# Full-height kv sums and a newly searched instruction order in a fused linear-attention and FFN kernel

## The chip, the cores and the metric

The kernel runs on one core of a Trainium2 chip. The metric is device time in microseconds (us); a median over several executions is given. Times of one kernel scatter by up to about 2 us either way, and the clock granted to TensorE, which differs from run to run, has a part in it: of eleven runs of the kernel before on one chip, the five with a mean clock of 0.989 or more took 262.73 to 264.61 us, the six with 0.985 or less 264.16 to 266.26. Kernels are compared by ratios: the mean time of one kernel's fast runs over that of the kernel before in the same rounds on the same chip, with a 95% interval. Such a ratio is not quite the ratio of the medians that stand beside it.

## The reference, cut to what matters

```python
def attn(q, k, v):                     # (8 batches, 8 heads, 576 tokens, 64)
    q_p, k_p = phi(q), phi(k)          # phi(x) = max(x + 1, min(exp(x), 1))
    kv  = einsum('bhsd,bhse->bhde', k_p, v)
    z   = k_p.sum(axis=2)
    return einsum('bhsd,bhde->bhse', q_p, kv) / (einsum('bhsd,bhd->bhs', q_p, z)[..., None] + 1e-6)
x = attn(q, k, v), as 4608 tokens x 512
out = (((x @ w1) * (x @ w2)) @ w3) @ w_out
```

All inputs and the output are float32. The 576 tokens of a batch are four tiles of 128 ("J") and a remainder of 64 ("R").

## The kernel before

The program is one list of short tokens, ORDER. Every engine executes its own instructions in the order in which the tokens emit them, so the list fixes what stands in front of what on each engine. Letters that this text uses:

- L, M, N: loads of k, q, v of a batch (`M1.2`: all of batch 1's q except the remainder). A gate such as `M1.2<E3` holds a load back until another has landed. B, C, E: loads of w1/w2, w_out and w3, cast to bf16 on the way, from the POOL (GpSimd) queue. The other loads are issued by SyncE (SP).
- x, y, z (for k) and X, Y, Z (for q): exp on ScalarE (ACT), min and max on VectorE (DVE). v: cast of v.
- K: one kv sum for four heads. A: the attention output of one batch, in parts. a, b: q transposes on TensorE (PE) and their copy.
- w: transposes of a w3 piece on PE and the copy out of PSUM, the memory that PE writes to here; a unit on PE waits until a bank of it is free. U, W: the product w3 @ w_out, halves and whole, with a copy at the end of W.
- F: one 128-column unit of the FFN (8 matmuls of 512 columns, a copy on ACT, a product on DVE). O, S: output matmuls and stores.
- A token that ends in "+" makes its copy on DVE in place of ACT. For K it meant, in this kernel, the half-height version; on the load of a remainder it means the POOL queue.

The two ways to form kv (cut):

```python
    def kv_half(b, g):
        ...
        for i in range(2):                      # two head pairs
            steps = [... four tiles, halves (0, 1) ...]
            steps.append((... remainder ..., (g,)))
            for n, (kk, vv, halves) in enumerate(steps):
                for r in halves:                # rows 0-63 into bank 0, rows 64-127 into bank 1
                    rows = slice(r * R, (r + 1) * R)
                    nc.tensor.matmul(kvp[:, r, i * W:(i + 1) * W], kk[rows], vv[rows], ...)
        nc.scalar.copy(out=kvf, in_=kvp[:, 0, 0:2 * W])
        nc.vector.tensor_tensor(out=kvs[b][...], in0=kvf, in1=kvp[:, 1, 0:2 * W], op=ALU.add)

    def kv_full(b, g):
        ...
        rows = slice(g * R, (g + 1) * R)
        for i in range(2):
            for j in range(NJ):                 # four 128-row tiles
                nc.tensor.matmul(kvp[:, 0, i * W:(i + 1) * W], kj[:, hp, j]..., vt[:, j, ...]...,
                                 start=(j == 0), stop=False)
            nc.tensor.matmul(kvp[:, 0, i * W:(i + 1) * W], kr[rows, i * P:(i + 1) * P],
                             vr[rows, 2 * i:2 * i + 2, :]..., start=False, stop=True)
```

A half-height unit is 18 matmuls of 64 rows, a copy and an add. A full-height one is 8 matmuls of 128 rows and 2 of 64, and one copy. Going from 128-row to 64-row matmuls and back is what the texts below call a change of (tiling) mode.

Of the kernel before, what the change touches and what calls it, by code (L numbers as in the profile page):

```python
# [13 lines left out]
P = 128  # L14
# [4 lines left out]
def kernel(  # L19
# [158 lines left out]

    kvs, qts, xns = {}, {}, {}

    def kv_half(b, g):


        kj, kr = ph["k", b]
        if g == 0:
            kvs[b] = att.tile([P, KC, 2, D + 1], BF16, tag="kv", name="kv")
        kvp = at_ps.tile([P, 2, 512], F32, tag="at", name="kvp")
        W = 2 * (D + 1)
        for i in range(2):
            hp = 2 * g + i  # L190
            steps = [(kj[:, hp, j].rearrange("p u d -> p (u d)"),
                      vt[:, j, 2 * hp:2 * hp + 2, :].rearrange("p h e -> p (h e)"), (0, 1))
                     for j in range(NJ)]
            steps.append((kr[:, i * P:(i + 1) * P],
                          vr[:, 2 * i:2 * i + 2, :].rearrange("p h e -> p (h e)"), (g,)))
            for n, (kk, vv, halves) in enumerate(steps):
                for r in halves:
                    rows = slice(r * R, (r + 1) * R)
                    nc.tensor.matmul(  # L199
                        kvp[:, r, i * W:(i + 1) * W], kk[rows], vv[rows],  # L200
                        start=(n == 0), stop=(n == (NJ if r == g else NJ - 1)))
        kvf = lr.tile([P, 2 * W], F32, tag="kvf", name="kvf")
        nc.scalar.copy(out=kvf, in_=kvp[:, 0, 0:2 * W])
        nc.vector.tensor_tensor(
            out=kvs[b][:, 2 * g:2 * g + 2].rearrange("p a u e -> p (a u e)"), in0=kvf,
            in1=kvp[:, 1, 0:2 * W], op=ALU.add)

    def kv_full(b, g):

        kj, kr = ph["k", b]  # L210
        if g == 0:
            kvs[b] = att.tile([P, KC, 2, D + 1], BF16, tag="kv", name="kv")
        kvp = at_ps.tile([P, 2, 512], F32, tag="at", name="kvp")
        W = 2 * (D + 1)
        rows = slice(g * R, (g + 1) * R)
        for i in range(2):
            hp = 2 * g + i
            for j in range(NJ):
                nc.tensor.matmul(kvp[:, 0, i * W:(i + 1) * W],
                                 kj[:, hp, j].rearrange("p u d -> p (u d)"),  # L220
                                 vt[:, j, 2 * hp:2 * hp + 2, :].rearrange("p h e -> p (h e)"),
                                 start=(j == 0), stop=False)
            nc.tensor.matmul(kvp[:, 0, i * W:(i + 1) * W], kr[rows, i * P:(i + 1) * P],
                             vr[rows, 2 * i:2 * i + 2, :].rearrange("p h e -> p (h e)"),
                             start=False, stop=True)
        return kvp[:, 0, 0:2 * W]
# [289 lines left out]
    def step(s):  # L516
# [20 lines left out]
        elif t == "U":  # L537
            wf_mm(b, 0)
            held["U", b] = True
        elif t == "W":  # L540
            wf_mm(b, 1 if ("U", b) in held else 2, alt)
        elif t in "LMN":
            name = "kqv"["LMN".index(t)]
            ins = load_qkv(name, src[name], b, i, alt)
            loaded(s, ins)
        elif t == "B":
            for ins in load_w12(b):
                loaded(s, ins)
        elif t == "C":
            loaded(s, load_wo(b))  # L550
        elif t == "E":
            loaded(s, load_w3(b))
        elif t in "xX":
            phi_exp("kq"["xX".index(t)], b, i)
        elif t in "yY":
            phi_min("kq"["yY".index(t)], b, i)
        elif t in "zZ":
            phi_max("kq"["zZ".index(t)], b, i)
        elif t == "v":
            v_unit(b, i, alt)  # L560
        elif t == "T":
            qt_load(b, i)
        elif t == "K":
            if alt:
                kv_half(b, i)
            else:
                kv_copy(b, i, kv_full(b, i))
        elif t == "A":
            nat_units(b, ((0, 1), (2, 3), (4,))[i])
        elif t == "D":  # L570
            xt_load(b, i)
        elif t == "P":
            xt_tr(b, i, alt)
        elif t == "a":
            held["a", b, i] = q_tr(b, i)
        elif t == "b":
            held["a", b, i](alt)
        elif t == "c":
            held["c", i] = kv_full(0, i)
        elif t == "d":  # L580
            first_kvz(i, held["c", i])
        elif t == "e":
            held["e", i] = first_nd(i, i < 2)
        elif t == "f":
            held["e", i][0]()
        elif t == "g":
            held["e", i][1]()
        elif t == "h":
            if i == 0:
                held["h"] = [f_open(0, 0), f_open(0, 1)]  # L590
            for f in range(2):
                for ps, w in zip(held["h"][f], (w1_sb, w2_sb)):
                    f_mm(0, f, ps, w, i)
        elif t == "i":
            f_close(0, i, *held["h"][i])
        elif t == "r":
            first_rest()
# [32 lines left out]
```

## Time and profile before

263.69 us (263.31 to 264.38, 3 runs).

| engine | busy us of 263.1 | what matters |
|---|---|---|
| PE | 240.0 | full from 58 us to the end; one wide gap, 47 to 52 us |
| DVE | 171.4 | not waited for after 58 us |
| ACT | 124.9 | executes in order; holds PSUM banks while it waits for a load |
| DMA | full to about 52 us | the casting weight queue and the loads of q, k, v share it |

Busy time alone would say that DVE and ACT have room and that PE has 23 us to spare. The view to trust is the one by stretches: it tells in which part of the time PE is full. Columns: stretch and its length, then busy us and instructions of PE, PE's weight loads, DVE, ACT and POOL, then clock, DMA share, GB/s.

```profile
60.00:258.00 198.00, 198.00 (x1399) 94.13 (x1393) 140.60 (x358) 94.57 (x158) 0.00 (x0) 1.00 0.68 177
```

PE is busy for 198.00 of 198.00 us. Here a microsecond of work taken from DVE or ACT is worth nothing, and one added to PE is paid. The groups that the change takes off DVE and ACT are these (busy us, mean ns, then the idle time before them):

```profile
L204 DVE TENSOR_TENSOR kv<-kvf,kvp 128x260 bf16<-128x260 f32 x13 | 5.5, 419 | 4.2 <-ACT kvf L203 4.2
L203 ACT COPY kvf<-kvp 128x260 f32<-128x260 f32 x13 | 4.9, 375 | 6.2 <-PE kvp L199 6.2
```

### The profile page before, as it was taken

The page shows a single profiled execution, that of the slowest core. Times are in us where ns is not written, and L with a number is a line of the kernel's source. Part 1 is how long each engine was busy: PE and PEld are TensorE (multiplying, and loading weights), DVE is VectorE, ACT ScalarE, POOL GpSimd, SP SyncE. Part 2 cuts the span into 40 slices and gives each one's busy share as a digit, 9 for nine tenths or more (in the row PEclk, how much of TensorE's full clock was granted, in tenths as well). Part 3 has the DMA queues.
Part 4 walks back from the last instruction along what each step waited for, and adds up shares of the span by engine and source line. Part 5 has one row for each costly group of instructions (what it writes and reads, how often), then busy time and mean ns, then how long its engine had stood idle before and what let it go on. Part 6 is the DMA issues. An engine that isn't in the chain of part 4 may idle for free.

```text
span 263.1 us, 4457 instructions
## 1 busy us (share of the span) xinstructions
PE 240.0 (91%) x1652; PEld 115.7 (44%) x1652; DVE 171.4 (65%) x431; ACT 124.9 (47%) x199; POOL 13.5 (5%) x30
## 2 busy tenths in 40 slices
PE   0467999399999999999999999999999999999993
PEld 0133544255544554454444544444444444444442
DVE  0495644465898996988798679669886624433341
ACT  1576521663885986497345743733242222323200
POOL 2075300000000000000000000000000000000000
PEclk9999999869999999999999999999999999999999
DMA  5999999957959989997999897993655411202033
GB/s 174 293 322 195 206 208 256 264 175 225 368 162 283 188 222 229 324 209 185 283 181 229 227 338 231 176 244 78 135 156 171 94 50 34 88 0 80 0 122 121
DMA packets 75045, 49.51 MB, mean 188 GB/s; under 512 B 39568, under 2 KB 69520, under 8 KB 75024
## 3 DMA queue, kind: packets, MB, share of 16 engines
q1 hardware_dynamic: 68448, 43.85, 62.1%
q0 software_dynamic: 6432, 5.24, 12.6%
q8 instruction: 13, 0.21, 0.3%
q10 hardware_dynamic: 144, 0.13, 0.1%
q14 instruction: 8, 0.07, 0.1%
HBM read 38.80 MB, written 9.44 MB: 183 GB/s over the span
## 4 chain that ended last, share of the span: by engine, by line
PE 83%; DMA 11%; SPq 2%; ACT 1%; POOL 1%; issue 1%; ACTq 0%
PE a_ps L371 24%; PE o_ps L390 23%; PE b_ps L371 23%; DMA q<-in_q_dram 5%; PE wf_ps L464 3%; PE kvp L199 3%; DMA w_sb<-in_moe_w_dram 3%; DMA k<-in_k_dram 3%; PE nd L265 3%; SPq L111 1%; PE xtp L285 1%; SPq L120 1%; PE w3p L454 1%; PE o_ps L417 1%; PE tp L309 1%
## 5 line engine op out<-in xcount | busy, mean ns | idle before, releaser
L371 PEld LDWEIGHTS <-w_sb 128*128 128x128 bf16 x576 | 54.3, 98 | 64.1 <-DMA w_sb<-in_moe_w_dram 0.7
L377 DVE TENSOR_TENSOR ab<-a_sb,b_ps 128x512 bf16<-128x512 f32 x72 | 49.0, 684 | 41.0 <-PE b_ps L371 35.5
L371 PE MATMUL a_ps<-xt,w_sb 128*128 128x512 bf16 x288 | 75.1, 380 | 0.0
L371 PE MATMUL b_ps<-xt,w_sb 128*128 128x512 bf16 x288 | 74.9, 379 | 0.2 <-DMA w_sb<-in_moe_w_dram 0.2
L376 ACT COPY a_sb<-a_ps 128x512 f32<-128x512 f32 x72 | 41.9, 585 | 61.8 <-PE a_ps L371 59.8
L390 PE MATMUL o_ps<-wf_sb,ab 128*128 128x512 bf16 x280 | 63.9, 379 | 0.0
L390 PEld LDWEIGHTS <-ab 128*128 128x128 bf16 x280 | 26.5, 98 | 30.5 <-DVE ab L377 0.2
L393 DVE COPY o_sb<-o_ps 128x512 f32<-128x512 f32 x20 | 13.8, 688 | 15.1 <-PE o_ps L390 15.1
L162 DVE SCALAR_TENSOR_TENSOR kj<-k,e 128x256 bf16<-128x256 f32 x64 | 23.5, 416 | 0.0
L162 DVE SCALAR_TENSOR_TENSOR qj<-q,e 128x256 bf16<-128x256 f32 x64 | 23.5, 416 | 0.1
L137 ACT ACTIVATE e<-q 128x1024 bf16<-128x1024 f32 x16 | 16.8, 1059 | 10.8 <-DMA q<-in_q_dram 10.8
L393 ACT COPY o_sb<-o_ps 128x512 f32<-128x512 f32 x15 | 8.8, 585 | 22.8 <-PE o_ps L390 18.5
L275 DVE TENSOR_TENSOR xn<-nd,r 128x512 bf16<-128x512 f32 x28 | 18.0, 685 | 0.0
L141 DVE TENSOR_SCALAR e<-e 128x1024 bf16<-128x1024 bf16 x32 | 13.1, 417 | 7.3 <-ACT e L137 7.3
L464 PE MATMUL wf_ps<-wo_sb,w3t 128*128 128x512 bf16 x64 | 17.1, 411 | 0.1
L137 ACT ACTIVATE e<-k 128x1024 bf16<-128x1024 f32 x16 | 16.9, 1057 | 0.3 <-DMA k<-in_k_dram 0.3
L171 ACT CAST vt<-v 128x1024 bf16<-128x1024 f32 x13 | 13.7, 1050 | 1.3 <-DMA v<-in_v_dram 1.3
L100 PE MATMUL warm<-zero 128*128 128x512 bf16 x12 | 4.2, 523 | 10.2 <-DVE zero L94 10.2
L141 DVE TENSOR_SCALAR er<-er 128x256 bf16<-128x256 bf16 x16 | 3.5, 218 | 9.2 <-ACT er L137 9.2
L464 PEld LDWEIGHTS <-w3t 128*128 128x128 bf16 x64 | 6.2, 104 | 7.1 <-issue 1.5
L199 PEld LDWEIGHTS <-kj 64*128 64x128 bf16 x208 | 6.6, 94 | 4.8 <-issue 4.2
L199 PE MATMUL kvp<-vt,kj 64*128 64x130 bf16 x208 | 8.7, 218 | 0.0
(79 smaller groups left out, 153.3 us busy)
## 6 DMA issues: line engine op xcount, KB each, us to landing
out_dram<-o_sb SPq DMA_DIRECT2D x31, 256.0 KB, 3.0
k<-in_k_dram SPq DMA_DIRECT2D x7, 1024.0 KB, 7.8
q<-in_q_dram SPq DMA_DIRECT2D x7, 1024.0 KB, 8.3
v<-in_v_dram SPq DMA_DIRECT2D x6, 1024.0 KB, 6.9
v<-in_v_dram SPq DMA_DIRECT2D x4, 512.0 KB, 8.1
w3b<-in_moe_w_dram POOLq DMA_DIRECT2D x8, 256.0 KB, 13.1
w_sb<-in_moe_w_dram POOLq DMA_DIRECT2D x8, 256.0 KB, 9.0
out_dram<-o_sb SPq DMA_DIRECT2D x9, 128.0 KB, 2.4
```

The lines of the kernel that those rows point to most:

```text
L137: nc.scalar.activation(out=e, in_=x, func=AF.Exp)
L141: nc.vector.tensor_scalar_min(out=e, in0=e, scalar1=1.0)
L162: nc.vector.scalar_tensor_tensor(out=out, in0=x, scalar=1.0, in1=e, op0=ALU.add, op1=ALU.max)
L171: copy_of(alt)(out=vt[:, :, 4 * i:4 * i + 4, 0:D], in_=raw["v", b].rearrange("p (h j d) -> p j h d", h=H, j=NJ)[:, :, 4 * i:4 * i + 4])
L199: nc.tensor.matmul(kvp[:, r, i * W:(i + 1) * W], kk[rows], vv[rows], start=(n == 0), stop=(n == (NJ if r == g else NJ - 1)))
L275: nc.vector.tensor_tensor(out=dst.rearrange("p (c u) e -> p u c e", u=2), in0=v4[:, :, :, 0:D], in1=r[0:n].unsqueeze(3).to_broadcast([n, 2 ...
L371: nc.tensor.matmul(ps, w[:, kc, f * P:(f + 1) * P], xt[:, 4 * c:4 * c + 4, kc, :], start=(kc == 0), stop=(kc == KC - 1))
L376: nc.scalar.copy(out=a_sb, in_=a_ps)
L377: nc.vector.tensor_mul(out=abs_[c][:, f, :], in0=a_sb, in1=b_ps)
L390: nc.tensor.matmul(o_ps, ab[:, f, m * P:(m + 1) * P], wf_sb[:, f, :], start=(f == 0), stop=(f == FC - 1))
L393: copy_of(alt)(out=o_sb, in_=o_ps)
L464: nc.tensor.matmul(wfs[i], w3ts[i][:, kc, :], wo_sb[:, kc, :], start=(kc == 0), stop=(kc == FC - 1))
```

## The change

Its intent: every kv unit as full-height matmuls with a single copy, which puts one copy in place of a copy and an add, and a new order, found by a search whose transfer rates came from traces in which two DMA queues work at once. The core of the diff (the order itself is 28 lines, cut):

```diff
-    def kv_half(b, g):
-        ...
-            if alt:
-                kv_half(b, i)
-            else:
-                kv_copy(b, i, kv_full(b, i))
+            kv_copy(b, i, kv_full(b, i), alt)
     ORDER (after the first w3 and FFN units)
-    i0.0 i0.1 x1.1 w1+ F0.2 F0.3 N1.3 w2+ y1.0 F0.4 N1.1 y1.1 F0.5 U1 N2.3 U0 W0+ E4 x1.2 W1 w3+
-    W2+ W3 M2.3 z1.0 X1.0 E5 M0.3 y1.2 z1.1 Y1.0 Z1.0 Z1.1 X1.1 Y1.1 M2.2 z1.2 F0.6 E6 w4 Z1.2
-    Z1.3 z1.3 F0.7 E7 w5 Z1.4 a1.0 v1.2+ b1.0 z1.4 U4 w6 W4 ...
+    x1.2 w1 Z1.4 x1.1 F0.2 y1.0 z1.0 M2.3+ F0.3 F0.4 B3 y1.1 w2 U0 F0.5 z1.1 N1.0 E4 U1 N2.3
+    X1.0 z1.2 W0+ N1.3+ w3+ X1.1 E5 W1+ y1.2 W2 Y1.0 Z1.0 Z1.1 v1.2+ W3 N1.1 F0.6 w4+ M2.2 F0.7
+    Y1.1 L2.3 a1.0 M3.3 w5+ b1.0 M0.3 z1.3 E6 U4 z1.4 w6 v1.0 W4+ E7 Z1.2 Z1.3 w7+ U5 W5 K1.0+ ...
-    GATES = "B0<M0.1 C0<L0.1 E0<L0.1 E4<N0.1 M1.2<E3 N1.0<B3"
+    GATES = "B0<L0.0 C0<L0.0 E0<N0.1 M1.2<E3 N1.0<B3"
```

More of the change, by code (lines that the diff above doesn't have):

```diff
@@ L179 @@
     kvs, qts, xns = {}, {}, {}
-    def kv_half(b, g):
-        kj, kr = ph["k", b]
-        if g == 0:
-            kvs[b] = att.tile([P, KC, 2, D + 1], BF16, tag="kv", name="kv")
-        kvp = at_ps.tile([P, 2, 512], F32, tag="at", name="kvp")
-        W = 2 * (D + 1)
-        for i in range(2):
-            hp = 2 * g + i
-            steps = [(kj[:, hp, j].rearrange("p u d -> p (u d)"),
-                      vt[:, j, 2 * hp:2 * hp + 2, :].rearrange("p h e -> p (h e)"), (0, 1))
-                     for j in range(NJ)]
-            steps.append((kr[:, i * P:(i + 1) * P],
-                          vr[:, 2 * i:2 * i + 2, :].rearrange("p h e -> p (h e)"), (g,)))
-            for n, (kk, vv, halves) in enumerate(steps):
-                for r in halves:
-                    rows = slice(r * R, (r + 1) * R)
-                    nc.tensor.matmul(
-                        kvp[:, r, i * W:(i + 1) * W], kk[rows], vv[rows],
-                        start=(n == 0), stop=(n == (NJ if r == g else NJ - 1)))
-        kvf = lr.tile([P, 2 * W], F32, tag="kvf", name="kvf")
-        nc.scalar.copy(out=kvf, in_=kvp[:, 0, 0:2 * W])
-        nc.vector.tensor_tensor(
-            out=kvs[b][:, 2 * g:2 * g + 2].rearrange("p a u e -> p (a u e)"), in0=kvf,
-            in1=kvp[:, 1, 0:2 * W], op=ALU.add)
     def kv_full(b, g):
@@ L470 @@
     ORDER = """
-    I1 L0.0 L0.3 M0.0 I0 M1.3 X0.0 x0.2 N0.0 y0.2 N0.3 z0.4 v0.0 M0.1 I2 L0.1 E0 E1 x0.0 X0.1
-    N0.1 Y0.0 Z0.0 B0 X1.2 Z0.1 y0.0 z0.0 z0.1 Y0.1 v0.2+ x0.1 H12 Y1.2 L1.3 B1 c0.0 B2 L1.2
-    Z0.2 a0.0 E2 b0.0 d0.0 e0.0 y0.1 Z0.3 z0.2 a0.1 b0.1+ z0.3 e0.1 v0.1 C0 E3 f0.1 w0+ f0.0
-    c0.1 C1 g0.1 d0.1 e0.2 f0.2 e0.3 g0.0 f0.3 x1.0 g0.2 g0.3 M1.2 B3 h0.0 h0.1 h0.2 N1.0 h0.3
-    i0.0 i0.1 x1.1 w1+ F0.2 F0.3 N1.3 w2+ y1.0 F0.4 N1.1 y1.1 F0.5 U1 N2.3 U0 W0+ E4 x1.2 W1 w3+
-    W2+ W3 M2.3 z1.0 X1.0 E5 M0.3 y1.2 z1.1 Y1.0 Z1.0 Z1.1 X1.1 Y1.1 M2.2 z1.2 F0.6 E6 w4 Z1.2
@@ L477 @@
-    Z1.3 z1.3 F0.7 E7 w5 Z1.4 a1.0 v1.2+ b1.0 z1.4 U4 w6 W4 v1.0 T1.1 a1.1 v1.1+ U5 L2.3 b1.1
-    N3.3 U6 K1.0+ X2.2 W5+ w7+ K1.1 W6 L2.2 A1.0 U7 x2.2 W7 A1.1 X2.0 O0.3 N2.2 Y2.0 Y2.2 X2.1
-    P1.1+ L3.3 P1.0 Z2.4 Y2.1 X0.2 O0.2+ L3.2 Z2.0 y2.2 M3.3 Z2.1 x2.0 z2.4 P1.3 y2.0 M3.2 P1.2
-    O0.1 x2.1 Z2.2 z2.0 x3.2 v2.0 O0.0+ y2.1 v2.2+ z2.1 Z2.3 T2.0 F1.0 N3.2 Y0.2 z2.2 Z0.4 F1.1
-    v2.1 K2.0+ T0.1 z2.3 x3.0 F1.2 F1.3 y3.0 K2.1+ y3.2 A1.2 F1.4 M4.2 D1.1 z3.0 X3.2 X3.0 Y3.2
-    F1.5 x3.1 A2.0 X3.1 F1.6 P2.0 v3.2 A2.1 v3.0 M4.3 z3.4 S0.3 y3.1 Z3.4 F1.7 Y3.1 T2.1 Y3.0
@@ L483 @@
-    P2.1 r0 z3.1 z3.2 z3.3 Z3.0 O1.1 v3.1 P2.2 L5.3 L4.2 Z3.1 Z3.2 L4.3 O1.3 Z3.3 M5.3 P2.3 X4.0
-    Y4.0 X4.2 K3.0+ F2.0 F2.1 N4.3 A2.2 T3.0 x4.0 S0.2 N4.2 Y4.2 F2.2 X4.1 y4.0 F2.3 S0.1 K3.1+
-    M6.3 F2.4 x4.1 z4.0 x4.2 Z4.0 y4.2 Z4.1 A3.0 y4.1 O1.2 F2.5 Y4.1 O1.0 M5.2 A3.1 S0.0 v4.1
-    P3.1 F2.6 P3.3+ z4.1 v4.0 P3.2 F2.7 z4.4 Z4.4 X5.0 Z4.2 S1.3 T3.1 P3.0 v4.2 Z4.3 z4.2 X5.2
-    O2.3+ Y5.0 D2.1 F3.0 z4.3 L5.2 X5.1 T4.0 A3.2 x5.0 S1.1 S1.2 N5.3 F3.1 N5.2 K4.0+ F3.2 Y5.1
-    x5.1 K4.1+ Z5.0 y5.1 T4.1 L6.2 F3.3 A4.0 O2.0 F3.4 y5.0 x5.2 A4.1 z5.0 L6.3 y5.2 D3.1 O2.1+
@@ L489 @@
-    Y5.2 F3.5 Z5.1 D4.0 S1.0 S2.3 v5.2 A4.2 M6.2 Z5.2 v5.0 F3.6 F3.7 Z5.4 x6.2 O3.3+ Z5.3 v5.1
-    z5.1 T5.1 z5.2 z5.3 O2.2 x6.0 F4.0 z5.4 X6.2 x6.1 T5.0 F4.1 F4.2 K5.0+ y6.0 y6.1 X6.0 Y6.0
-    K5.1+ S2.1 S2.2 z6.0 F4.3 y6.2 S2.0 F4.4 N6.2 F4.5 O3.2 L7.2 Z6.0 X6.1 A5.0 Z6.1 z6.4 z6.1
-    F4.6 Y6.1 v6.1+ F4.7 z6.2 A5.1 S3.2 O3.0+ M7.2 O4.0 v6.0 z6.3 S3.3 Z6.2 O4.1+ L7.3 X7.0 N6.3
-    A5.2 Z6.3 v6.2 x7.0 x7.2 X7.1 O4.3+ O3.1 D5.0 Y6.2 S3.0 O4.2+ T6.0 y7.0 y7.2 x7.1 Y7.0 K6.0+
-    F5.0 F5.1 z7.4 N7.2 F5.2 Z6.4 N7.3 K6.1+ S4.3 z7.0 T6.1 z7.1 F5.3 A6.0 v7.2+ y7.1 F5.4 S4.1
@@ L495 @@
-    D5.1 F5.5 Y7.1 D4.1 A6.1 M7.3 F5.6 F5.7 S4.0 Z7.0 D6.0 z7.2 X7.2 O5.2+ Z7.1 O5.0 v7.0+ Z7.2
-    Y7.2 O5.1+ Z7.3 T7.0 S3.1 A6.2 S5.1 Z7.4 S5.0 T7.1 F6.0 v7.1 K7.0+ D6.1 z7.3 F6.1 F6.2 K7.1+
-    S4.2 O5.3+ S5.3 A7.0 F6.3 S5.2 F6.4 A7.1 F6.5 F6.6 F6.7 A7.2 D7.0 O6.0 O6.3 D7.1 S6.0 O6.1+
-    F7.0 F7.1 O6.2+ S6.2 F7.2 F7.3 F7.4 F7.5 F7.6 F7.7 O7.1+ F8.0 O7.0 S6.1 F8.1 F8.2 S6.3 F8.3
-    F8.4 F8.5 S7.0 F8.6 F8.7 S7.1 O8.1+ O8.0+ S8.0 O7.3+ O7.2+ S7.3 S8.1 O8.3+ S7.2 S8.3 Q8.2
+    I1 L0.0 N0.3+ M1.3 x0.0 y0.0 L0.3 v0.2 M0.0 I0 z0.0 x0.2 X1.2 y0.2 z0.1 Y1.2 M0.1 I2 X0.0
@@ new lines @@
+    z0.4 N0.0 Y0.0 v0.0+ N0.1 H12 Z0.0 c0.0 L0.1 Z0.1 X0.1 Y0.1 E0 x0.1 B0 y0.1 C0 a0.0 d0.0
+    L1.2 b0.0 e0.0 L1.3 z0.2 v0.1 z0.3 E1 w0 Z0.2 f0.0 Z0.3 e0.1 a0.1 b0.1 B1 B2 E2 c0.1 d0.1
+    e0.2 E3 f0.1 g0.0 g0.1 f0.2 e0.3 h0.0 g0.2 M1.2 f0.3 h0.1 C1 g0.3 x1.0 h0.2 h0.3 i0.0 i0.1
+    x1.2 w1 Z1.4 x1.1 F0.2 y1.0 z1.0 M2.3+ F0.3 F0.4 B3 y1.1 w2 U0 F0.5 z1.1 N1.0 E4 U1 N2.3
+    X1.0 z1.2 W0+ N1.3+ w3+ X1.1 E5 W1+ y1.2 W2 Y1.0 Z1.0 Z1.1 v1.2+ W3 N1.1 F0.6 w4+ M2.2 F0.7
+    Y1.1 L2.3 a1.0 M3.3 w5+ b1.0 M0.3 z1.3 E6 U4 z1.4 w6 v1.0 W4+ E7 Z1.2 Z1.3 w7+ U5 W5 K1.0+
@@ new lines @@
+    v1.1 X2.2 U6 a1.1 K1.1 X2.0 W6 b1.1+ L2.2 x2.2 Y2.2 X2.1 A1.0 T1.1 y2.2 U7 Y2.0 N3.3 W7 A1.1
+    O0.3 N2.2 P1.1 Z2.0 x2.0 P1.0+ Z2.4 Z2.1 O0.0 Y2.1 P1.2+ X0.2 Z2.2 x2.1 O0.1 y2.1 y2.0 Y0.2
+    P1.3 z2.0 L3.3 z2.1 v2.2 Z2.3 O0.2 L3.2 z2.4 x3.2 z2.2 F1.0 v2.0 M3.2 A1.2 F1.1 K2.0+ v2.1+
+    x3.0 y3.0 Z0.4 z2.3 F1.2 X3.0 F1.3 T2.0 K2.1+ x3.1 z3.0 y3.2 N3.2 F1.4 X3.2 D1.1 z3.1 T0.1
+    A2.0 F1.5 X3.1 F1.6 A2.1 Y3.0 P2.0 Y3.1 F1.7 z3.4 v3.2+ P2.2 r0 S0.3 P2.1 T2.1 Z3.0 L4.3
+    Y3.2 y3.1 M4.2 v3.0+ x4.2 Z3.1 z3.2 Z3.4 L5.3 Z3.2 M4.3 v3.1 z3.3 L4.2 O1.3 Z3.3 O1.1 M5.3
@@ new lines @@
+    X4.0 F2.0 S0.0 K3.0 X4.2 F2.1 X4.1 F2.2 M6.3 x4.0 T3.0 y4.0 N4.3+ Y4.2 M5.2 F2.3 K3.1+ A2.2
+    v4.2+ F2.4 x4.1 S1.3 z4.0 S0.1 N4.2 F2.5 A3.0 O1.0 T3.1 P2.3 Y4.0 P3.0+ A3.1 S0.2 z4.1 F2.6
+    O1.2 P3.3+ Z4.0 Z4.1 F2.7 Y4.1 P3.2 y4.2 Z4.4 Z4.2 P3.1 Z4.3 y4.1 O2.3+ z4.2 A3.2 v4.1 S1.1
+    v4.0 L5.2 F3.0 z4.4 T4.1 z4.3 X5.0 T4.0 F3.1 N5.2 x5.2 x5.0 F3.2 X5.1 D3.1 Y5.0 K4.0+ Z5.0
+    L6.2 X5.2 N5.3 F3.3 L7.3 y5.2 Y5.2 S1.0 K4.1+ F3.4 O2.0 L6.3+ Z5.4 Y5.1 A4.0 F3.5 A4.1 F3.6
+    F3.7 Z5.1 z5.4 O2.2 v5.0 Z5.2 D2.1 Z5.3 v5.2+ x5.1 v5.1 O3.3 y5.1 D4.0 S1.2 N6.3+ x6.0 y5.0
@@ new lines @@
+    S2.3 z5.0 x6.2 M6.2 O2.1+ z5.1 F4.0 O3.2+ N6.2 F4.1 T5.0 X6.0 x6.1 y6.0 z5.2 S2.0 Y6.0 A4.2
+    F4.2 X6.2 z5.3 F4.3 K5.0+ F4.4 K5.1+ v6.2 S2.2 z6.0 z6.1 F4.5 X6.1 M7.2 A5.0 S2.1 y6.2 y6.1
+    v6.0 Y6.1 F4.6 L7.2 S3.3 T5.1 O3.0 F4.7 z6.2 S3.2 A5.1 D5.0 z6.3 z6.4 S3.0 Z6.0 M7.3 x7.0
+    y7.0 Z6.1 O4.3 Y6.2 O4.1 K6.0+ Z6.2 O4.0+ X7.0 v6.1 Z6.3 T6.0 O3.1 S4.1 N7.2 Z6.4 x7.2 O4.2
+    A5.2 K6.1+ F5.0 y7.2 z7.4 Y7.0 F5.1 z7.0 F5.2 z7.1 F5.3 x7.1 Z7.0 A6.0 S4.0 N7.3 F5.4 S4.3
+    S4.2 D4.1 F5.5 A6.1 v7.2 v7.0+ F5.6 F5.7 v7.1 Z7.1 X7.1 Y7.1 y7.1 Z7.2 z7.2 Z7.3 z7.3 O5.2
@@ L500 @@
+    S3.1 O5.0+ O5.1+ K7.0 K7.1+ O5.3 T6.1 D6.0 X7.2 D5.1 F6.0 F6.1 T7.0 A7.0 S5.0 F6.2 F6.3 A7.1
+    F6.4 F6.5 Y7.2 S5.3 S5.2 Z7.4 F6.6 F6.7 D7.0 S5.1 A6.2 O6.0 F7.0 O6.3 D6.1 F7.1 O6.2+ F7.2
+    O6.1 F7.3 S6.2 T7.1 F7.4 A7.2 S6.1 S6.0 F7.5 S6.3 F7.6 F7.7 O7.2+ D7.1 O7.3 O7.1 F8.0 O7.0+
+    F8.1 F8.2 F8.3 S7.1 F8.4 S7.3 F8.5 F8.6 S7.0 S7.2 F8.7 O8.0 O8.3+ S8.0 S8.3 O8.1 S8.1 Q8.2
     """
-    GATES = "B0<M0.1 C0<L0.1 E0<L0.1 E4<N0.1 M1.2<E3 N1.0<B3"
+    GATES = "B0<L0.0 C0<L0.0 E0<N0.1 M1.2<E3 N1.0<B3"
```

## The prediction

> **What bounds the kernel now.** I read first the engine shares and the slices on the page, then PE's waits, then the order of time around the one wide gap, then the DMA queues there.
>
> ```profile
> PE 240.0 (91%) x1652; PEld 115.7 (44%) x1652; DVE 171.4 (65%) x431; ACT 124.9 (47%) x199; POOL 13.5 (5%) x30
> PE   0467999399999999999999999999999999999993
> PEclk9999999869999999999999999999999999999999
> DMA  5999999957959989997999897993655411202033
> ```
>
> A slice is 6.6 us. PE is full from slice 8 to the end; what is missing lies in the first three slices (loads come in) and in slice 7, where the clock of the next two slices also drops. The list of waits by engine has PE idle after the start for one thing of size:
>
> ```profile
> PE tp L309 <- ACT w3t L455: 4.5, 1, 4.5
> ACT e L137 <- DMA q<-in_q_dram: 10.8, 3, 5.8
> ```
>
> From 58 us to 258.7 us no matmul waits: start to start, the 512-column ones stand at 0.216 us throughout (770 such distances, none over 0.228). So after 58 us the time is PE's own work plus some 4.4 us of last copy and store, and every microsecond of PE work added there is paid in full. The gap itself, in the timelines of SP, PE and ACT:
>
> ```profile
> 34.81 0.37 SPq L120 DMA_DIRECT2D q<-in_q_dram  x1
> 46.79 0.61 PE L454 MATMUL w3p<-ident,w3b 128*128 128x128 bf16 x8
> 51.95 1.01 PE L309 MATMUL tp<-ident,qj 128*128 128x128 bf16 x8 [4.55 <-ACT w3t L455]
> 48.52 2.00 ACT L137 ACTIVATE e<-q 128x1024 bf16<-128x1024 f32 x2 [4.84 <-DMA q<-in_q_dram]
> 50.89 1.01 ACT L455 COPY w3t<-w3p 128x1024 bf16<-128x1024 bf16 x1
> ```
>
> Batch 1's q (1 MB, M1.2) is issued at 34.81, when the fourth w3 piece has landed (its gate), and lands at 48.49. ACT executes in order and stands in front of that exp; the copies behind it, which free PSUM for PE, wait too. PE restarts 51.95 - 48.49 = 3.5 us after the landing. In two-microsecond windows the granted clock is 0.68 (50-52), 0.50 (52-54 and 54-56), 0.62 (56-58): about 5.6 us of work at half rate, 2.8 us lost. The gap costs 4.55 + 2.8 = 7.3 us in all; that is the largest thing a new order could win.
>
> Why q takes 13.7 us, from the DMA queues in the stretch 34 to 45 us (packets, MB, share of 16 engines):
>
> ```profile
> q0 software_dynamic: 1943, 1.85, 101.4%
> q1 hardware_dynamic: 613, 0.63, 19.9%
> ```
>
> The casting weight queue (q0, sizes as written in bf16, so 3.7 MB read) holds most of the engines; q gets 0.63 MB. It lands when the weights are through (last w3 piece 48.25).
>
> **What the Trainium skill says.** "DMA: Bandwidth & Descriptors", section "Queues, rings and completion order": each DMA engine takes the queues with work in turn, a packet at a time. The trace agrees in direction: two queues in work, and the one with packets near 1 KB moves 0.63 MB beside 1.85 MB. "TensorE: Matmul & The Clock Gate", part 1: about 3.4 us without work halve the clock until about 3.4 us of sustained work, in a window that runs free of the kernel. Agrees: 4.55 us idle, then 0.50. "TensorEngine Tiling (Array Packing)", "Key Properties": changing the tiling mode drains TensorE. Agrees: a 64-row matmul after a full one starts 0.311 us after it instead of 0.216, so 0.095 us for going in, and about as much coming out.
>
> **The change, part 1: kv.** Half-height (L199, K1.0) and full (L219/L223, K1.1), both after the clock is back, from PE's timeline:
>
> ```profile
> 59.54 0.40 PE L199 MATMUL kvp<-vt,kj 64*128 64x130 bf16 x8
> 59.78 0.22 PE L199 MATMUL kvp<-vr,kr 64*128 64x130 bf16 x1
> 59.78 0.44 PE L199 MATMUL kvp<-vt,kj 64*128 64x130 bf16 x8
> 60.06 0.22 PE L199 MATMUL kvp<-vr,kr 64*128 64x130 bf16 x1
> 60.21 1.04 PE L464 MATMUL wf_ps<-wo_sb,w3t 128*128 128x512 bf16 x4
> 61.53 0.39 PE L219 MATMUL kvp<-vt,kj 128*128 128x130 bf16 x4
> 61.86 0.23 PE L223 MATMUL kvp<-vr,kr 64*128 64x130 bf16 x1
> 62.02 0.40 PE L219 MATMUL kvp<-vt,kj 128*128 128x130 bf16 x4
> 62.35 0.23 PE L223 MATMUL kvp<-vr,kr 64*128 64x130 bf16 x1
> 62.51 1.04 PE L464 MATMUL wf_ps<-wo_sb,w3t 128*128 128x512 bf16 x4
> ```
>
> By starts, 18 half matmuls take 60.21 - 59.54 = 0.67 us plus 0.10 for going in: 0.77. Ten full ones take 62.51 - 61.53 = 0.98, although they are fewer: the row tiles let two halves run at once (30 ns per half matmul, 57 ns per full one, so no gain in streaming), and the full version still ends each head pair on a 64-row remainder, so it changes mode four times instead of twice. Before has 13 half units, 11 alone and one pair (146.84 to 147.97 = 1.13, plus 0.10): 11 x 0.77 + 1.23 = 9.7 us. After, 13 x 0.98 = 12.7. Counted from the order, mode changes rise from 77 to 105. **PE gains 3.0 us of work**, all of it after 58 us.
>
> On the other side go 13 ACT copies (0.375 us each, 4.9 us) and 13 DVE adds (0.419, 5.5 us); in come single copies, by the new order 11 on DVE (about 4.6 us at the add's duration) and 3 on ACT, one of which existed (so 0.75 us new). ACT and DVE lose some 5 us together. PE waits for neither after 58 us, so this is worth about 0.
>
> **Part 2: the order.** (a) Start. Batch 0's v remainder moves to the POOL queue, the small remainders go first on SP, the large halves follow back to back. The small ones land slowly (in before 3.0 MB landed by 14.21). If the four large pieces run at the 0.36 MB/us of 12 to 16 us instead of the 0.27 of 5 to 11, I estimate the fifth half at 12.5 to 14 us, and the whole DMA chain 0 to 1.8 us earlier; I take 1.0. (b) Weights. Same 20 pieces of 1.33 us; the first weights for the FFN come before the second w3 piece, which is nice for the first FFN matmul. But the first w3 transposes (w0) now stand ahead of half of the batch 0 chain on PE, and their copy on ACT ahead of the four Ln/Exp pairs (1.3 us each); I find the first FFN chunk no earlier than before. (c) The gap. M1.2 keeps its gate, and the same pieces precede it, so q should land near 48.5 - 1.0 = 47.5. Yet the new order puts both of its exps on ACT right after unit F0.5's copy, ahead of the copies of W2 and W3. PE then runs W2, W3, F0.6 and w4's transposes and must stop: F0.7's bank (four in rotation) is the one that W2's copy frees. In before F0.7 and w5 were already done when PE stopped. So PE restarts after two exps and one copy, 1.06 + 1.0 + 0.6 = 2.6 us after landing: 50.1, against 51.95, which is -1.85, with F0.7 (1.73) and w5 (0.45) still to do, +2.2. Net +0.35. Idle would be near 4.5 to 5 us, so the clock probably drops again; since the window runs free it may last shorter or not happen: I put -0.8 on that. (d) From there to the end PE should stay full, as the searches both manage; 0 to 1 us of new stalls, say +0.5.
>
> **Sum.** +3.0 (kv) +0.35 (gap) -0.8 (clock) +0.5 (stalls) = +3.0: 266.7. Against that stands that this order was searched with rates from traces, and that its author may know the landing of q better than I; a fourth of the weight goes to the rival below, and the number is 265.3.
>
> **Rivals.** *The gap is gone.* If q lands by about 40 us, as the early place of its exps suggests that the search believed, 7.3 us go and 3.0 come: 259 to 260. For it: the name of the change. Against it: the gate and the share of the queue are as before. *The half-height sums did cost something hidden*, a PSUM pair held through copy and add: then PE would show waits on kvp; it shows none, 0 gain. *A worse start*: ACT is the chain from w0 on, and if the first w3 piece lands at 20 us again, F0.7 and more slip behind q: 268 to 270. *ACT becomes the bound*: ten o_sb copies move from DVE to ACT (10 x 0.585 = 6 us), but ACT is 47% busy: no more than 1 us.
>
> **Range and chances.** 259.3 to 269.0 spans both main cases. Faster by over 2% needs 258.4, the gap gone and the start better too, in spite of 3.0 us more on PE: 0.06. Slower by over 2% needs 269.0, a gap longer by 3 us or more: 0.11. The rest, 0.83.
>
> **What would show it.** Right: 1,548 or so matmul records instead of 1,652 (13 x 8 fewer); full kv units near 0.98 us each; PE busy up about 3 us once clock effects are taken off; a PE gap near 45 to 50 us put down to ACT, with the exp of q waiting for the DMA; q landing within 2 us of the last w3 piece. Wrong: q landing by 40 us and no gap; or full kv units near 0.6 us; or new PE waits after 60 us.

## The result, and the profile after

266.70 us (266.43 to 267.23, 4 runs) against 264.03 us of before; ratio 1.0102, interval 1.0066 to 1.0139. The change makes the kernel about 1% slower, which counts as the same at the 2% mark.

The page of the changed kernel, engine shares and slices:

```profile
PE 244.7 (93%) x1530; PEld 119.2 (45%) x1548; DVE 166.0 (63%) x421; ACT 126.6 (48%) x196; POOL 21.7 (8%) x42
PE   0758999599999999999999999999999999999994
PEclk9975999899999999999999999999999999999999
```

PE gained 4.7 us of busy time, not all of it work, since a matmul at half clock counts as longer (0.63 us in place of 0.38 for 512 columns; slices 2, 3 and 7); DVE lost 5.4. ACT even gained 1.7: the new order moves output copies from DVE to it. (18 matmul records are missing in this trace; the weight loads, 1548, show the true number.) Slice 7 still has the gap, and the clock still dips after it. In the stretch after 60 us PE is full again, the missing records aside:

```profile
60.00:258.00 198.00, 197.08 (x1262) 94.14 (x1276) 134.84 (x347) 94.48 (x153) 4.37 (x6) 1.00 0.63 171
```

The groups of the single copy, which stand in place of copy and add:

```profile
L203 DVE CAST kv<-kvp 128x260 bf16<-128x260 f32 x11 | 4.7, 424 | 1.7 <-PE kvp L197 1.2
L203 ACT CAST kv<-kvp 128x260 bf16<-128x260 f32 x3 | 1.1, 375 | 5.7 <-PE kvp L197 5.7
```

The gap, in the timelines of SP, PE and ACT (start us, length us, what; in brackets the idle time before and what ended it):

```profile
33.57 0.37 SPq L120 DMA_DIRECT2D q<-in_q_dram  x1
46.18 0.61 PE L428 MATMUL w3p<-ident,w3b 128*128 128x128 bf16 x8
49.74 1.12 PE L345 MATMUL a_ps<-xt,w_sb 128*128 128x512 bf16 x4 [2.95 <-ACT wf_sb L441]
47.21 2.00 ACT L137 ACTIVATE e<-q 128x1024 bf16<-128x1024 f32 x2 [9.33 <-DMA q<-in_q_dram]
49.12 1.05 ACT L441 CAST wf_sb<-wf_ps 128x512 bf16<-128x512 f32 x2
```

ACT stands 9.33 us before the exp of q, which lands at 47.19 us. PE waits for F0.7's bank, which the copy of W2 frees; that copy comes behind both exps. And a full-height unit among its neighbours, from PE's timeline:

```profile
58.36 0.39 PE L193 MATMUL kvp<-vt,kj 128*128 128x130 bf16 x4
58.68 0.23 PE L197 MATMUL kvp<-vr,kr 64*128 64x130 bf16 x1
58.84 0.40 PE L193 MATMUL kvp<-vt,kj 128*128 128x130 bf16 x4
59.18 0.23 PE L197 MATMUL kvp<-vr,kr 64*128 64x130 bf16 x1
59.34 1.04 PE L438 MATMUL wf_ps<-wo_sb,w3t 128*128 128x512 bf16 x4
```

By starts the unit takes 59.34 - 58.36 = 0.98 us. The four full matmuls take 0.32 us to the first remainder, of which 0.17 are the first three (57 ns each) and 0.15 the fourth: some 0.10 us more for going into the 64-row mode. The remainder then takes 0.16, again 0.10 more than 57 ns, for coming out.

Where the time went, between the two traces: PE's last matmul starts at 258.41 us before and at 260.42 after, 2.0 us later. That is made of a restart after the gap 2.2 us earlier (51.95 to 49.74), 2.2 us of work that is still to do there and was done before (F0.7 and w5), 1.1 us less lost to the half clock (5.59 us of it after PE's restart before, 3.41 after, half of each), and 3.0 us of kv: -2.2 + 2.2 - 1.1 + 3.0 = 1.9. The stretch behind the last matmul is 0.8 us shorter in this trace (4.7 and 3.9); no run isolates that.

### The profile page after: what moved, and what is told of

Its sections match the earlier page's. It is cut to its first block, busy times and chain, and to the rows that moved or that the text cites. A ratio compares the mean times of both kernels' runs of the same rounds, so it can differ in the third digit from the quotient of the medians.

```text
span 264.3 us, 4223 instructions
## 1 busy us (share of the span) xinstructions
PE 244.7 (93%) x1530; PEld 119.2 (45%) x1548; DVE 166.0 (63%) x421; ACT 126.6 (48%) x196; POOL 21.7 (8%) x42
## 4 chain that ended last, share of the span: by engine, by line
PE 79%; DMA 15%; SPq 2%; issue 1%; ACT 1%; POOL 0%; ACTq 0%
PE o_ps L364 23%; PE a_ps L345 22%; PE b_ps L345 22%; DMA q<-in_q_dram 5%; DMA w3b<-in_moe_w_dram 4%; PE kvp L193 3%; DMA v<-in_v_dram 3%; PE wf_ps L438 3%; DMA w_sb<-in_moe_w_dram 3%; PE nd L239 3%; PE kvp L197 2%; PE xtp L259 1%; SPq L111 1%; SPq L120 1%; PE o_ps L391 1%
## 5 line engine op out<-in xcount | busy, mean ns | idle before, releaser
L345 PE MATMUL b_ps<-xt,w_sb 128*128 128x512 bf16 x288 | 76.2, 384 | 0.0
L364 PE MATMUL o_ps<-wf_sb,ab 128*128 128x512 bf16 x266 | 63.2, 379 | 0.7
L367 ACT COPY o_sb<-o_ps 128x512 f32<-128x512 f32 x25 | 14.6, 585 | 37.2 <-PE o_ps L364 33.6
L141 DVE TENSOR_SCALAR e<-e 128x1024 bf16<-128x1024 bf16 x32 | 13.1, 423 | 16.4 <-ACT e L137 16.4
L137 ACT ACTIVATE e<-q 128x1024 bf16<-128x1024 f32 x16 | 16.8, 1057 | 11.8 <-DMA q<-in_q_dram 11.7
L438 PE MATMUL wf_ps<-wo_sb,w3t 128*128 128x512 bf16 x61 | 15.0, 379 | 0.3 <-issue 0.2
L193 PE MATMUL kvp<-vt,kj 128*128 128x130 bf16 x128 | 13.1, 227 | 0.0
L100 PE MATMUL warm<-zero 128*128 128x512 bf16 x12 | 5.1, 617 | 8.2 <-DVE zero L94 8.2
L171 ACT CAST vt<-v 128x1024 bf16<-128x1024 f32 x12 | 12.5, 1049 | 0.0
L111 POOL DMA_DIRECT2D v32r<-in_v_dram x8 | 5.7, 722 | 67.5 <-DMA k<-in_k_dram 54.8
L367 DVE COPY o_sb<-o_ps 128x512 f32<-128x512 f32 x10 | 6.8, 687 | 6.1 <-PE o_ps L364 6.1
L193 PEld LDWEIGHTS <-kj 128*128 128x128 bf16 x128 | 8.7, 101 | 4.3 <-issue 0.3
## 6 DMA issues: line engine op xcount, KB each, us to landing
w_sb<-in_moe_w_dram POOLq DMA_DIRECT2D x8, 256.0 KB, 10.2
```

Source lines behind the costliest of these rows:

```text
L137: nc.scalar.activation(out=e, in_=x, func=AF.Exp)
L141: nc.vector.tensor_scalar_min(out=e, in0=e, scalar1=1.0)
L171: copy_of(alt)(out=vt[:, :, 4 * i:4 * i + 4, 0:D], in_=raw["v", b].rearrange("p (h j d) -> p j h d", h=H, j=NJ)[:, :, 4 * i:4 * i + 4])
L345: nc.tensor.matmul(ps, w[:, kc, f * P:(f + 1) * P], xt[:, 4 * c:4 * c + 4, kc, :], start=(kc == 0), stop=(kc == KC - 1))
L364: nc.tensor.matmul(o_ps, ab[:, f, m * P:(m + 1) * P], wf_sb[:, f, :], start=(f == 0), stop=(f == FC - 1))
L367: copy_of(alt)(out=o_sb, in_=o_ps)
```

## The experiments

Two theories stood against each other. **Mine:** the full-height kv unit costs PE 3.0 us by its changes between 128-row and 64-row mode, and the new order is worth about nothing, because its gap is set by the landing of q. **The rival:** the kv change is neutral, and the order lost by its start and its gap. A second question was whether the gap is a matter of order on ACT, of q's landing, or of loads in general. Twelve kernels ran, all with correct results, all with five rounds.

### The changed kernel again

> The changed kernel unaltered, as a base for its neighbours on the same chip: 266.7 us, ratio 1.010 to before, as recorded. If the ratio came out under 1.005 the difference to be explained would be mostly the clock's chance (the granted clock of single runs ranged from 0.974 to 0.994).

266.79 us, ratio 1.0072 (1.0034 to 1.0110). The two readings of the changed kernel, 1.0102 and this one, agree within their intervals; a difference of 0.3% between two sets of runs is not to be explained. Its trace shows the same gap: 3.12 us, with PE back at 49.97 us and 3.4 us at half clock.

### Each part alone

The new order with half-height sums:

```diff
-            kv_copy(b, i, kv_full(b, i), alt)
+            if (b, i) != (1, 1):
+                kv_half(b, i)
+            else:
+                kv_copy(b, i, kv_full(b, i))
```

> The new order, but the 13 kv units that before summed in halves again as half-height sums with copy and add. Theory (the full-height kv costs TensorE 3.0 us by its mode changes, and the new order is worth about nothing in total): 3.0 us off, 263.7 us, ratio 0.999, matmul distances of a kv unit back at 0.57 to 0.77 us. Rival (the kv change is neutral and the new order is what lost, by its start and its gap): 266 to 267 us, ratio 1.010.

264.01 us, ratio 0.9975 (0.9934 to 1.0016), 2.8 us under the changed kernel on the same chip by medians. The new order alone is as fast as the old one, within the interval.

The old order with full-height sums:

```diff
-            if alt:
-                kv_half(b, i)
-            else:
-                kv_copy(b, i, kv_full(b, i))
+            kv_copy(b, i, kv_full(b, i), alt)
```

> The old order, with the 13 half-height units as full-height ones and one DVE copy: the kv part of the change alone. Theory: 3.0 us on top of before, 267.0 us, ratio 1.011, the gap near 47 to 52 us unchanged. Rival: 263.5 to 264.5 us, ratio 1.000.

267.56 us, ratio 1.0116 (1.0080 to 1.0151): 3.1 us more (1.16% of 264.5). The gap is where it was, as the wait list of PE shows (total, times, longest):

```profile
PE tp L309 <- ACT w3t L455: 4.4, 1, 4.4
```

So the loss is the kv part, in both orders, and the rival falls.

### What in the full-height unit costs the time

If the changes of mode are the cost, they can be halved or removed with ten matmuls per unit left as they are. First halved: the two remainders together at the end, the second head pair in the second bank.

```diff
-                nc.tensor.matmul(kvp[:, 0, i * W:(i + 1) * W], ...)   # 4 x full
-            nc.tensor.matmul(kvp[:, 0, i * W:(i + 1) * W], kr[rows, ...], vr[rows, ...], ...)
+                nc.tensor.matmul(kvp[:, i, 0:W], ...)                 # 4 x full
+        for i in range(2):
+            nc.tensor.matmul(kvp[:, i, 0:W], kr[rows, ...], vr[rows, ...], ...)
-        return kvp[:, 0, 0:2 * W]
+        return kvp[:, :, 0:W]
```

> The changed kernel, but the two 64-row remainders of a unit come together after the eight full matmuls (the second head pair sums in the second bank of its PSUM pair), so two mode changes per unit and not four. Theory: 13 x 0.2 = 2.6 us less, 264.1 us, ratio 1.000, a unit near 0.75 us. Rival (a mode change costs nothing by itself): no change, 266.7 us.

264.33 us, ratio 1.0015 (0.9992 to 1.0039). A unit runs from 58.85 to 59.61, 0.76 us:

```profile
58.85 0.62 PE L193 MATMUL kvp<-vt,kj 128*128 128x130 bf16 x8
59.40 0.29 PE L198 MATMUL kvp<-vr,kr 64*128 64x130 bf16 x2
59.61 0.82 PE L439 MATMUL wf_ps<-wo_sb,w3t 128*128 128x512 bf16 x3
```

Then removed: the remainder as a 128-row matmul too. The 64 rows that belong to the other four heads meet zeros in v.

```diff
-    vr = wpool.tile([P, H // 2, D + 1], BF16)
+    vr = wpool.tile([P, 2, H // 2, D + 1], BF16)     # zeroed once; half g real in vr[:, g]
-            copy_of(alt)(out=vr[:, :, 0:D], in_=raw["vr", b]...)
+            for hh in range(2):
+                rows = slice(hh * R, (hh + 1) * R)
+                copy_of(alt)(out=vr[rows, hh, :, 0:D], in_=raw["vr", b][rows]...)
-            nc.tensor.matmul(..., kr[rows, i * P:(i + 1) * P], vr[rows, 2 * i:2 * i + 2, :]..., ...)
+            nc.tensor.matmul(..., kr[:, i * P:(i + 1) * P], vr[:, g, 2 * i:2 * i + 2, :]..., ...)
```

> The changed kernel, but the 64-row remainder of each head pair becomes a 128-row matmul against a v remainder whose other half is zeros (two masked tiles, two half-height copies per batch in place of one copy). The kv unit then has ten full-height matmuls and no change of tiling mode. Theory (the extra cost of the full-height unit is its four mode changes, near 0.1 us each): a unit falls from 0.97 to 10 x 0.057 = 0.57 us, 13 x 0.40 = 5.2 us less, 261.5 us, ratio 0.991. Rival (the cost is the number of weight loads or the 130-column matmuls themselves): the unit stays above 0.85 us and the time above 265.5.

261.39 us, ratio 0.9912 (0.9881 to 0.9943). A unit runs from 58.64 to 59.21, 0.57 us:

```profile
58.64 0.39 PE L197 MATMUL kvp<-vt,kj 128*128 128x130 bf16 x4
58.87 0.22 PE L201 MATMUL kvp<-vr,kr 128*128 128x130 bf16 x1
58.92 0.39 PE L197 MATMUL kvp<-vt,kj 128*128 128x130 bf16 x4
59.15 0.22 PE L201 MATMUL kvp<-vr,kr 128*128 128x130 bf16 x1
59.21 1.03 PE L442 MATMUL wf_ps<-wo_sb,w3t 128*128 128x512 bf16 x4
```

Ten matmuls in each of the three versions, with four, two and no changes of mode: 0.98, 0.76 and 0.57 us. That is about 0.10 us per change. It is not a cost of each 64-row matmul, since two of them together cost half of what two apart do, nor one of weight loads or columns, which are alike in all three. The same sums without a change of mode are cheaper than the half-height version was (0.67 us and 0.10 for going in).

### What holds the gap

One move in the order: batch 1's q exps go behind the copies of W2, W3, F0.6 and F0.7 on ACT, and its transposes behind more w3 work on PE.

```diff
-    X1.0 z1.2 W0+ N1.3+ w3+ X1.1 E5 W1+ y1.2 W2 Y1.0 Z1.0 Z1.1 v1.2+ W3 N1.1 F0.6 w4+ M2.2 F0.7
-    Y1.1 L2.3 a1.0 M3.3 w5+ b1.0 M0.3 z1.3 E6 U4 z1.4 w6 v1.0 W4+ E7 Z1.2 Z1.3 w7+ U5 W5 K1.0+
+    z1.2 W0+ N1.3+ w3+ E5 W1+ y1.2 W2 v1.2+ W3 N1.1 F0.6 w4+ M2.2 F0.7 L2.3 M3.3 w5+ M0.3 z1.3
+    E6 X1.0 U4 X1.1 z1.4 w6 Y1.0 Z1.0 v1.0 W4+ E7 Z1.1 Y1.1 w7+ U5 a1.0 Z1.2 W5 Z1.3 b1.0 K1.0+
```

> The new order with one move: batch 1's two q exps and the DVE work on them go behind the copies of W2, W3, F0.6 and F0.7, and the q transposes of batch 1 go behind w5, U4, w6, W4, w7 and U5 on TensorE. Theory (TensorE stops only because ScalarE stands before the exp of q, which lands at 47.2 us): the gap of 2.95 us is closed and the clock drop after it (1.7 us lost in the trace) does not come: 266.7 - 4.6 = 262.1 us, ratio 0.993, range 261.3 to 263.3. Rival (the kernel is bound by the loads up to 58 us, so the wait only moves to the next tile that is late): 265.5 to 266.7 us with a gap of 2 us or more elsewhere before 65 us.

262.01 us, ratio 0.9923 (0.9881 to 0.9966). In PE's timeline F0.7 follows w4's transposes at once, and w5 follows F0.7:

```profile
45.17 0.61 PE L428 MATMUL w3p<-ident,w3b 128*128 128x128 bf16 x8
45.62 1.03 PE L345 MATMUL a_ps<-xt,w_sb 128*128 128x512 bf16 x4
46.48 1.03 PE L345 MATMUL b_ps<-xt,w_sb 128*128 128x512 bf16 x4
47.34 0.61 PE L428 MATMUL w3p<-ident,w3b 128*128 128x128 bf16 x8
```

q lands no earlier (its exps run from 47.16 us), but PE has other work until it is ready. What is left of the wait is 0.7 us on a q tile and 0.2 on a v tile. The granted clock of the profiled run is 1.0, so the dip is gone from it too, and so is the half clock in the start, which both traces of the changed kernel had. That is not so in every run: of the six, three had a clock of 0.999 or 1.0 (261.61 to 262.14 us) and three 0.978 to 0.984 (261.87 to 264.25 us); where those lost it, no trace shows. The loads as such did not bound this stretch.

The other cure: q earlier, order untouched.

```diff
-    GATES = "... M1.2<E3 N1.0<B3"
+    GATES = "... M1.2<B1 N1.0<B3"
```

> The changed kernel with one gate moved: batch 1's q load (M1.2) is issued when the second quarter of w1 and w2 has landed (27.8 us), not when the fourth w3 piece has (33.4 us). Theory: q lands before 43 us, the exp no longer waits when TensorE needs W2's bank, the gap goes, the weights behind it come up to 2.7 us later and are still in time: 262 to 263 us, ratio 0.994. Rival (q only lands when the weight queue has drained, whenever it is issued): q still near 46 to 47 us, 266 us or more.

261.95 us, ratio 0.9916 (0.9887 to 0.9946). q is issued at 28.86 us and lands at 41.87, and the gap is gone. ACT still waits for it, but earlier than PE needs the copies behind it:

```profile
41.89 2.00 ACT L137 ACTIVATE e<-q 128x1024 bf16<-128x1024 f32 x2 [4.53 <-DMA q<-in_q_dram]
```

The last w3 piece lands at 49.78 us, so q does not have to wait until the weight queue is through, and the rival falls. One part of the expectation was missed: the weights did not all come in time, and PE waits once, for 1.5 us, for the second half of w_out.

The profiled run is 0.9 us longer than fill_gap's (spans of 260.7 and 259.8 us), which may be the trace of it; the medians do not differ. Both cures win 1.5 to 1.8% of the time over the changed kernel; the gap is where the landing of q meets the place of its exp on ACT, and either end can be moved.

### Both causes at once

> Both cures at once on the changed kernel: the exps moved behind the copies, and the masked full-height remainder. Theory: they add up, as one is a wait before 58 us and the other TensorE's own work after it: 266.7 - 4.6 - 5.2 = 256.9 us, ratio 0.973, range 256 to 259. Rival (the second half has other limits, the loads or DVE, that the slower kv unit hid): 259.5 us or more, with TensorE waits after 60 us.

257.68 us, ratio 0.9757 (0.9733 to 0.9781). The edit is fill_gap's order with masked_rest's matmul. The gains add: the reordering takes 0.014 to 0.016 from the ratio with each of three forms of kv (full, masked and, below, half). PE's last two waits of any size are these, at 52 and 56 us; after 60 us there is only one of 0.2 us.

```profile
PE tp L287 <- DVE qj L164: 0.7, 1, 0.7
PE kvp L197 <- ACT vt L173: 0.6, 1, 0.6
```

> The new order with half-height sums (order_half) and with the exps moved as in fill_gap. Theory (the two causes are independent and add): 264.0 - 4.6 = 259.4 us, ratio 0.982, some 1.7 us slower than fill_masked, since a half-height unit still changes mode twice. Rival (half-height sums cost nothing beside the masked ones): within 0.6 us of fill_masked, 257.7.

259.71 us, ratio 0.9830 (0.9792 to 0.9868): fill_gap's order with half-height sums. It is 0.7% slower than fill_masked, so the half-height version is not the best either.

### The start

In the changed kernel the first w3 transposes, w0, stand in front of half of batch 0's attention on PE, and they wait for a load. Moved behind the first FFN units, with its copy on DVE in place of ACT:

```diff
-    ... z0.3 E1 w0 Z0.2 f0.0 ...        ... i0.0 i0.1 x1.2 w1 ...
+    ... z0.3 E1 Z0.2 f0.0 ...           ... i0.0 i0.1 x1.2 w0+ w1 ...
```

> The changed kernel, but the first w3 transposes (w0, which wait for the first w3 piece) and their copy go behind the first FFN chunk, just ahead of w1, with the copy on VectorE. Theory (TensorE's restart is set by q's landing plus two exps and a copy, so what is won before the gap is lost in it): the first chunk ends 1.3 to 2 us earlier in the trace, the gap grows by as much, the time stays: 266.7 us, ratio 1.008, within 0.6 us of the changed kernel. Rival (the worse start is part of the loss): 1.3 to 2 us faster, 265 us.

267.85 us, ratio 1.0122 (1.0083 to 1.0162). No gain, as the theory has it, but the reasoning was only half tested. The first FFN units ended 0.6 us earlier, not 1.3 to 2 us. This is the start of the transposes behind them, in the changed kernel and then in this one:

```profile
29.30 0.61 PE L428 MATMUL w3p<-ident,w3b 128*128 128x128 bf16 x8
```

```profile
28.74 1.06 PE L428 MATMUL w3p<-ident,w3b 128*128 128x128 bf16 x16
```

PE ran at half clock from 16.8 to 27.0 us of this trace (the changed kernel's recorded trace shows the same from 16.4 to 26.6). The start is full of small waits, but they don't settle it: in fill_gap's trace, with the same order up to there as the changed kernel and waits of up to 1.4 us, the clock stays full. The gap grew from 2.95 to 3.34 us. The median lies 1.1 us above the changed kernel's, outside the 0.6 us that I had allowed; the intervals overlap, and whether this kernel is really slower stays open.

With the gap gone the start should count. The next kernel is fill_masked with w0 moved, and with a few w3 units put ahead of batch 1's attention so that PE does not run into q and v:

```diff
-    w7+ U5 a1.0 Z1.2 W5 Z1.3 b1.0 K1.0+ v1.1 X2.2 U6 a1.1 K1.1 X2.0 W6 b1.1+ ... A1.0 ... U7 ... W7 A1.1 O0.3
+    w7+ U5 Z1.2 W5 Z1.3 U6 a1.0 b1.0 K1.0+ v1.1 X2.2 W6 a1.1 U7 b1.1+ K1.1 X2.0 ... W7 A1.0 ... O0.3 A1.1
```

> The kernel with both cures (fill_masked), with w0 moved as in late_w0, and with U6 ahead of batch 1's first q transposes, W6 and U7 ahead of its second kv unit and W7 and O0.3 between the attention units, so that the earlier start does not run into q or v. Theory: without the gap the start counts, 1 to 1.7 us less than fill_masked: 256.3 us, ratio 0.970. Rival (the weights' landing times then hold TensorE, or q does): 257.3 us or more, with TensorE waits on a weight load or a kj, qj or vt before 60 us.

255.36 us, ratio 0.9674 (0.9635 to 0.9714), 3.3% under before. This kernel changed two things, so one more separates them: the later moves alone.

> fill_masked_start changed two things at once; this kernel keeps only the second (U6 ahead of batch 1's first q transposes, W6, U7, W7 and O0.3 between kv and attention units) and leaves w0 where it was. Theory (once the gap is gone the start counts, so w0's move brought most of the 2.2 us): between the two, near 257.0 us, ratio 0.973. Rival (the moves alone removed the waits on qj and vt of 0.7 and 0.6 us in fill_masked and brought nearly all): 255.4 to 256 us, ratio 0.968.

256.70 us, ratio 0.9708 (0.9677 to 0.9739). It lies between the two: of 0.0083 in the ratio, 0.0049 came with the moves and 0.0034 (0.9 us) with w0. So w0's move did not bring most of it, as the theory has it, nor the moves nearly all, as the rival has it. The intervals of the neighbours overlap, so the split is rough.

## Why the prediction was right, point by point

The range held the result. The single number was 1.4 us too low, and the steps say why. That the sum before the last step, 266.7 us, is the median that was measured is partly luck: it was counted from 263.69 us, which became 264.03, and its terms, as the traces have them below, make 1.9 us where the medians differ by 2.7.

- **kv, +3.0 us.** Right in size. By PE's starts the 13 units took 9.65 us before and 12.7 after. order_half (2.8 us by medians) and full_old_order (3.1 us) show it in the time, and rest_last and masked_rest show that the changes of mode are its cause.
- **ACT and DVE relieved, worth 0.** Right: by the groups, the kv copies and adds fell by 4.2 us on ACT (4.9 + 0.4 to 1.1) and by 0.8 on DVE (5.5 to 4.7), and full_old_order, which has that and the full-height matmuls alone, still lost 3.1 us, all that PE's own work costs. Most of the 5.4 us that DVE lost are output copies that the order moved to ACT (13.8 to 6.8 us on DVE), and no time came of them either.
- **q near 47.5 us.** It landed at 47.19, with the last w3 piece at 47.98. The gate and the pieces ahead of it were the same, so the landing was too, except that the first weight load was issued 1.35 us earlier (13.15 against 14.50 us). The reason given, that q lands when the weights are through, does not hold: in early_q it landed 7.9 us before the last of them. What stayed alike is the time that it takes beside the weight queue, 13.0 to 13.7 us in the traces of before, the changed kernel, fill_gap and early_q. Nor do 613 packets beside 1943 look like equal turns; the trace shows only that the queues shared the engines.
- **Restart at 50.1 after two exps and a copy.** It was 49.74, released by W2's copy, as forecast. Idle was 2.95 us and not 4.5 to 5: PE came to w4 later than I had it. The half clock in the start explains part: fill_gap's trace, without it, starts w4 at 45.17 us in place of 46.18, and traces of neighbours with this order have gaps of 3.1 to 4.0 us. That term was mis-sized, and it has no effect on the end, which hangs on q.
- **Clock, -0.8.** -1.1 in the trace; it differs from run to run. (The slices of before in which the clock drops are 7 and 8, not the two after 7.)
- **New stalls after 60 us, +0.5.** None: the stretch from 60 to 258 us is full.
- **The fourth of the weight for "the gap is gone".** This is the step that failed. The sum before it was 266.7 us, which is what was measured; I moved it to 265.3 (a fourth of the weight on 259 to 260 would give 264.9, so that step was also miscounted) because the name of the change promised rates from traces of two queues. The trace of before already had q's rate beside the weight queue (13.7 us for 1 MB), and nothing in the diff changed that. The evidence in the view should have outweighed the intent in the title.

The rival of a worse start (268 to 270 us) did not come: PE's start was slow, but it lay ahead of the gap, and what was lost there the gap took up. That is consistent with late_w0 and fill_masked_start; late_w0 gained nothing, yet moved the start by only 0.6 us, so it is not a sharp test.

## What to carry to other kernels

Count a matmul unit by the distances between starts, neighbours included, and not by the number of its matmuls: here 18 were cheaper than 10, until the 10 stopped changing the tiling mode, for which a remainder padded with zeros to full height was enough. An instruction that waits for a load on an in-order engine holds every buffer behind it, so put it behind the copies that the busiest engine needs, or issue its load earlier. And where one engine is full from some point to the end, only two things move the time: its own work after that point, and when it gets there.

## What the Trainium skill lacked or had wrong

- "TensorEngine Tiling (Array Packing)", "Key Properties" and "When to Use Tiling": a change of tiling mode drains TensorE, but no cost is given, and row tiling is recommended where the contraction is 64 or less. Here ten matmuls took 0.98, 0.76 and 0.57 us with four, two and no changes, about 0.10 us each, so a 64-row remainder among full-height matmuls did best when padded with zeros to 128 rows.
- "TensorE: Matmul & The Clock Gate", "Back-to-back issue gap": for streams of weight load and matmul it gives about 81 ns at 128 columns and 131 ns at 512. Here such streams ran at 57 ns with 130 columns and at 216 ns with 512 throughout, close to what it gives for a single matmul. Its part 1 lets the clock drop after about 3.4 us of idling; here a wait of 2.95 us (3.40 without the transposes that precede it) was followed by 3.41 us at half clock, and in the start of the same trace one of 1.52 us, the longest there since the clock was full, by 10.2 us of it, so less was enough. It did not always come: a wait of 1.83 us in fill_masked's start was followed by none.
- "DMA: Bandwidth & Descriptors", "Queues, rings and completion order": turns by packet are stated, but not what they mean for a plain load beside a casting queue with work in hand. Here 1 MB took 13.0 to 13.7 us from issue to landing beside it, in four traces, and 5.5 us (batch 2's q, issued at 51.38 us in the kernel before) once it was through.
